# Attention and a low-rank mixer MLP: from two phases in turn to one woven pass

## The chip, the cores and the metric

The kernel runs on one core of a Trainium2 chip. The metric is the device time of one execution in microseconds (us), as the median over several executions. TensorE does the matmuls, VectorE and ScalarE read their results, GpSimd and SyncE here mostly start transfers. In the profile lines these are PE (matmuls), PEld (loads of a matmul's stationary operand, "weights"), DVE, ACT, POOL and SP. A line number such as L215 is that of the kernel that was profiled.

## The reference

The batch is 8; each has 12 heads of 448 rows and 64 columns. The head outputs, side by side, are the 448 x 768 input of a mixer.

```python
def rmsnorm(x, g):
    return x / np.sqrt(np.mean(x * x, axis=-1, keepdims=True) + 1e-06) * g
q_n, k_n = rmsnorm(q, g_q), rmsnorm(k, g_k)
attn = softmax(q_n @ k_n.T / 8)             # per batch and head, 448 x 448
x = concat_heads(attn @ v)                  # 448 x 768
u = x + ((x.T @ U) @ V).T                   # U 448 x 32, V 32 x 448: mixes rows
out = u + np.maximum(u @ w_ch1, 0) @ w_ch2  # 768 -> 3072 -> 768
```

Inputs and output are 32-bit floats; both kernels multiply in bf16 and accumulate in 32 bits.

## The kernel before

There are two phases. Attention of all 8 batches writes its result, transposed, to a scratch tensor in device memory. Then the weights are loaded and the MLP of all batches runs. A scheduler orders the instructions from their dependences and buffers.

```python
# phase 1, for each batch (rmsnorm: Square, sum, Copy, reciprocal, Sqrt, multiply)
for h in range(H):
    for (src, gs, tg) in [(qnb, g_qs, "qT"), (knb, g_ks, "kT")]:
        ... # 4 transposes of 112x64, then ScalarE copies with the gain
    avT = psum3.tile([D + 1, S], FP32, tag="avT")
    for ki in range(NSP):                                       # 4 key tiles of 112
        nc.tensor.matmul(sc, knT[:, ki*SP:(ki+1)*SP], qnT, start=True, stop=True)
        nc.scalar.activation(sce, sc, AF.Exp, scale=scal)       # 112 x 448
        nc.tensor.matmul(avT, va_all[:, ki, h, :], sce, ...)    # output transposed, 65 x 448
    nc.vector.reciprocal(den, avT[D:D + 1, :])                  # one row of 448
    nc.gpsimd.partition_broadcast(denb, den)
    nc.vector.tensor_mul(oT, avT[:D, :], denb)
    nc.sync.dma_start(x_scratch[b, h*D:(h+1)*D, :], oT)
# phase 2: load and cast the weights, then for each batch
#   read xT back, transpose it, mix, w1 and Relu, w2 and add, transpose, store
... # cut
```

The softmax here doesn't subtract the row's maximum and nothing guards it: scores larger than these inputs give would overflow.

## Time and profile before

| what | value |
|---|---|
| time, median of 4 | 1168.05 us |
| attention, from the slices | to about 590 us |
| weights arrive and TensorE has gaps | 590 to 730 us |
| one MLP batch, period in the timeline | 63 us |
| busy share of TensorE, VectorE, ScalarE | 86%, 52%, 43% |

First, the slices on the page of the kernel before. Each digit is the busy share of one fortieth of the span, in tenths. PEclk is the clock that the throttle's records grant.

```profile
PE   0888788788988899999744996999999999999997
DVE  3688989998788769667754121330212212130302
ACT  3677877777676665666400421004040312112130
PEclk9999999999999999999996898899999999999998
```

Attention is the first half: all three engines are busy together. The MLP is the second, and TensorE is alone. The chain of work that ended last, followed back over the whole span, on the same page:

```profile
PE 69%; ACT 9%; DMA 8%; issue 7%; DVE 5%; POOL 1%; SPq 0%; POOLq 0%; ACTq 0%; DVEq 0%
```

The timeline of TensorE gives its real speed. The columns are start, length, engine, line, operation, output and inputs, shapes, and how many were merged. The first line is from attention, the others from the MLP.

```profile
407.10 1.81 PE L109 MATMUL avT<-sce,va_all 112*65 112x448 bf16 x4
...
858.56 1.30 PE L184 MATMUL ph_6153<-uTb,w1b 128*128 128x448 bf16 x6
859.70 1.30 PE L184 MATMUL ph_6161<-uTb,w1b 128*128 128x448 bf16 x6
```

In the MLP six matmuls of 448 columns start every 1.14 us, 189 ns each. In attention the first three of the four shown start 380 and 373 ns apart, about 375 ns each (the fourth came later). So attention runs at half speed. The PEclk row prints 9s there because the trace holds no clock record before 617 us; the spacing of back-to-back matmuls is the safer reading. The Trainium skill, "TensorE: Matmul & The Clock Gate", Part 1, describes the two speeds, 1.2 and 2.4 GHz, and says that sustained activity lifts the clock. By these rates I estimate 373 and 187 ns for 448 columns, which agrees with the spacings.

One group of VectorE is large (columns: line, engine, operation, tiles, shapes, count; busy us and mean ns; idle time before and who ended it):

```profile
L111 DVE RECIPROCAL den<-avT 1x448 f32<-1x448 f32 x96 | 281.9, 2944 | 80.3 <-PE avT L109 79.1
```

### The profile page before, as it was taken

How to read it: one execution, taken by the hardware profiler on the slowest of the kernel's cores; microseconds unless marked ns; L12 is line 12 of the kernel's file. 1: busy time of each engine (PE TensorE's matmuls, PEld its weight loads, DVE VectorE, ACT ScalarE, POOL GpSimd, SP SyncE). 2: the span in 40 equal slices, each digit the busy share in tenths (PEclk: the TensorE clock that was granted, in tenths of full speed). 3: DMA queues.
4: the chain of work that ended last, by engine and by line, in shares of the span. 5: the costliest groups of instructions: out<-in, count | busy, mean ns of one | idle time of the engine just before them, and what ended most of it. 6: DMA issues, size and time to landing. Idle time of an engine off the chain costs nothing.

```text
span 1165.7 us, 11492 instructions
## 1 busy us (share of the span) xinstructions
PE 1004.5 (86%) x4424; PEld 457.6 (39%) x4424; DVE 601.6 (52%) x483; ACT 495.7 (43%) x847; POOL 94.3 (8%) x122
## 2 busy tenths in 40 slices
PE   0888788788988899999744996999999999999997
PEld 0333233333333333333221443455555555555553
DVE  3688989998788769667754121330212212130302
ACT  3677877777676665666400421004040312112130
POOL 0012312211111111111110000000000000000000
PEclk9999999999999999999996898899999999999998
DMA  9567766243260000000075334011010202010101
GB/s 179 96 105 129 127 117 117 53 96 58 45 120 8 13 10 12 13 12 8 12 260 191 109 109 127 18 42 41 1 48 1 71 1 71 1 48 1 48 1 48
DMA packets 153703, 74.79 MB, mean 64 GB/s; under 512 B 133904, under 2 KB 146224, under 8 KB 152880
## 3 DMA queue, kind: packets, MB, share of 16 engines
q1 hardware_dynamic: 153648, 74.06, 27.7%
q8 instruction: 34, 0.56, 0.2%
q14 instruction: 21, 0.17, 0.0%
HBM read 57.52 MB, written 16.52 MB: 64 GB/s over the span
## 4 chain that ended last, share of the span: by engine, by line
PE 69%; ACT 9%; DMA 8%; issue 7%; DVE 5%; POOL 1%; SPq 0%; POOLq 0%; ACTq 0%; DVEq 0%
PE po L192 18%; PE sc L106 13%; PE avT L109 13%; DMA wf<-in_moe_w_ch_dram 7%; PE pt L97 6%; ACT sce L108 4%; PE ph L176 3%; ACT tT L99 2%; PE ot L198 2%; DVE w2b L136 1%; ACT L77 1%; ACT L108 1%; DVE ob L79 1%; DVE den L111 1%; DVE w1b L132 1%
## 5 line engine op out<-in xcount | busy, mean ns | idle before, releaser
L111 DVE RECIPROCAL den<-avT 1x448 f32<-1x448 f32 x96 | 281.9, 2944 | 80.3 <-PE avT L109 79.1
L108 ACT ACTIVATE sce<-sc 112x448 bf16<-112x448 f32 x384 | 200.0, 542 | 158.3 <-PE sc L106 115.3
L192 PE MATMUL po<-hT,w2b 128*128 128x448 bf16 x1152 | 231.5, 356 | 13.1 <-DVE w2b L136 12.9
L109 PE MATMUL avT<-sce,va_all 112*65 112x448 bf16 x384 | 196.1, 571 | 46.4 <-ACT sce L108 43.8
L106 PE MATMUL sc<-tT 64*112 64x448 bf16 x384 | 217.1, 599 | 14.2 <-ACT sce L108 13.1
L195 DVE TENSOR_TENSOR ofin<-po,uTb 128x448 bf16<-128x448 f32 x48 | 29.9, 625 | 312.2 <-PE po L192 312.2
L184 PEld LDWEIGHTS <-w1b 128*128 128x128 bf16 x1152 | 113.3, 99 | 125.6 <-DVE w1b L132 17.5
L192 PEld LDWEIGHTS <-w2b 128*128 128x128 bf16 x1152 | 110.3, 98 | 115.7 <-DVE w2b L136 19.9
L97 PE MATMUL pt<-ident,ob 112*64 112x112 bf16 x768 | 103.4, 292 | 40.1 <-DVE ob L79 31.4
L106 PEld LDWEIGHTS <-tT 64*112 64x112 bf16 x384 | 61.2, 178 | 168.1 <-issue 160.0
L113 POOL PARTITION_BROADCAST denb<-den x96 | 86.4, 900 | 461.6 <-DVE den L111 461.5
L97 PEld LDWEIGHTS <-ob 112*64 112x64 bf16 x768 | 74.3, 159 | 121.2 <-PE sc L106 42.5
L109 PEld LDWEIGHTS <-va_all 112*65 112x65 bf16 x384 | 51.3, 146 | 102.4 <-issue 85.1
L115 DVE TENSOR_TENSOR oT<-avT,denb 64x448 bf16<-64x448 f32 x96 | 59.2, 617 | 18.2 <-POOL denb L113 16.8
L99 ACT ACTIVATE tT<-pt,g_ks 64x448 bf16<-64x448 bf16 x96 | 59.7, 622 | 8.0 <-PE pt L97 4.3
L74 DVE TENSOR_REDUCE ssq<-sq 112x48 f32<-112x3072 f32 x16 | 53.0, 3311 | 19.1 <-ACT sq L72 19.1
L99 ACT ACTIVATE tT<-pt,g_qs 64x448 bf16<-64x448 bf16 x96 | 59.5, 620 | 3.0 <-PE pt L97 1.9
L79 DVE TENSOR_TENSOR ob<-t,ssq 112x3072 bf16<-112x3072 f32 x16 | 53.2, 3325 | 1.4 <-ACT ssq L77 1.4
L136 DVE CAST w2b<-wf 128x768 bf16<-128x768 f32 x24 | 13.4, 560 | 65.6 <-DMA wf<-in_moe_w_ch_dram 65.6
L176 PE MATMUL ph<-Wb,xb 112*128 112x448 bf16 x192 | 44.2, 368 | 1.2 <-DVE uTb L178 0.6
L72 ACT ACTIVATE sq<-t 112x3072 f32<-112x3072 f32 x16 | 44.1, 2754 | 0.0
L199 DVE CAST osb<-ot 112x512 f32<-112x512 bf16 x48 | 33.1, 690 | 21.1 <-PE ot L198 21.1
(420 smaller groups left out, 599.4 us busy)
## 6 DMA issues: line engine op xcount, KB each, us to landing
t<-in_q_dram SPq DMA_DIRECT2D x32, 336.0 KB, 5.1
t<-in_k_dram SPq DMA_DIRECT2D x32, 336.0 KB, 5.3
vt<-in_v_dram SPq DMA_DIRECT2D x32, 336.0 KB, 5.8
out_dram<-osb SPq DMA_DIRECT2D x32, 336.0 KB, 4.2
wf<-in_moe_w_ch_dram SPq DMA_DIRECT2D x6, 1536.0 KB, 6.7
wf<-in_moe_w_ch_dram SPq DMA_DIRECT2D x24, 384.0 KB, 3.0
x_scratch<-oT SPq DMA_DIRECT2D x96, 56.0 KB, 1.9
xT<-x_scratch SPq DMA_DIRECT2D x8, 672.0 KB, 4.8
```

Of the source, the lines that this page charges most:

```text
L79: nc.vector.tensor_tensor(ob, t, ssq.rearrange("p a h -> p a h ()").to_broadcast([SP, NSP, H, D]), AluOpType.mult)
L97: nc.tensor.transpose(pt[:, si * SP:(si + 1) * SP], src[:, si, h, :], ident[:SP, :SP])
L99: nc.scalar.activation(tT, pt, AF.Copy, scale=gs)
L106: nc.tensor.matmul(sc, knT[:, ki * SP:(ki + 1) * SP], qnT, start=True, stop=True)
L108: nc.scalar.activation(sce, sc, AF.Exp, scale=scal)
L109: nc.tensor.matmul(avT, va_all[:, ki, h, :], sce, start=(ki == 0), stop=(ki == NSP - 1))
L111: nc.vector.reciprocal(den, avT[D:D + 1, :])
L113: nc.gpsimd.partition_broadcast(denb, den)
L115: nc.vector.tensor_mul(oT, avT[:D, :], denb)
L176: nc.tensor.matmul(ph, xb[:, si, dti * P:(dti + 1) * P], Wb[:, si, :], start=(si == 0), stop=(si == KS - 1))
L184: nc.tensor.matmul(ph1, w1b[:, dti, hti * P:(hti + 1) * P], uTb[:, dti, :], start=(dti == 0), stop=(dti == KD - 1))
L192: nc.tensor.matmul(po, w2b[:, hti, dti * P:(dti + 1) * P], hT[:, hti, :], start=(hti == 0), stop=(hti == KH - 1))
```

## The change

The intent is to keep TensorE working on the MLP while the other engines serve attention. Attention of batch b+2 is cut into pieces, and these are placed by hand between chunks of six MLP matmuls of batch b. To fit, most pieces were rewritten: two heads at once in scores and transposes; the value product turned round, so that its output needs no scratch tensor (the mixing transposes it by matmuls against the identity); the mixing done in its low-rank form and the second MLP product turned round too, so that the output needs no transposes; 1/rms as exp(-0.5 ln(.)), from the one table that also serves the softmax; weights cast by the transfers. Two batches share the row tiles, so an even batch's MLP works on 384 rows and the next on 512. The diff, cut to its core:

```diff
-    # two phases, ordered by the scheduler
+    nc.scalar.preload_act_table_set("natural_log_exp_and_others")
+    def stats(t):                       # one tile t: four heads of q and k
+        ...  # Square on ScalarE, sums on VectorE
+        nc.scalar.activation(rs, rs, AF.Ln, bias=eps)
+        nc.scalar.activation(rs, rs, AF.Exp, scale=-0.5)
+    def scores(p, kcs):                 # p: a pair of heads
+        for kc in kcs:
+            for hh in range(2):
+                pp = slice(hh * D, (hh + 1) * D)       # rows 0-63 or 64-127
+                nc.tensor.matmul(sc[:, hh, 0:S], kT[pp, kc*SP:(kc+1)*SP], qT[pp, :], ...)
+    def values(p, hh):
+        for i, off in enumerate(OFFS[par]):            # 4 tiles of 128 query rows
+            for kc in range(NJ):
+                nc.tensor.matmul(o[:, i, :], E[:, hh, c:c + P], va[:, hl, kc, :], ...)
+        nc.vector.reciprocal(rec, o[:, :, D])          # 128 x 4
+        ...                                            # scale into x3 and xs
+    def mlp(b):                         # yields after each chunk of six matmuls
+        ...
+    def attention(b):                   # pieces, in this order, for each pair p
+        # start(p): scores 0, 1, exp 0 | values(p-1, 0) | exp 1 | [even p: stats(t+1)]
+        # scores 2, 3, exp 2 | values(p-1, 1) | exp 3 | [odd p: scale(t+1)] | transposes(p+1)
+    def weave(fill, total, items):      # spreads the items evenly over MLP columns
+        ...
+    with tc.manual_schedule():
+        ...                             # batch 0's attention alone
+        for b in range(B):
+            fill, total = mlp(b), volume(b % 2)
+            if b == 0:
+                first = attention(1)
+                for _, piece in first[:6] + mixing(0):
+                    piece()
+                weave(fill, 24 * 384, first[6:])
+                weave(fill, total - 24 * 384 - 3000, attention(2))
+            else:
+                weave(fill, total * 0.84, attention(b + 2) ...)
+            weave(fill, total * 0.13, mixing(b + 1))
```

## The prediction

> **What bounds the kernel now.** Two phases run in turn. In the 40 slices, attention fills the first half (to about 590 us), then weights load and the MLP runs to the end. The chain of waits is 69% TensorE. The timeline shows two TensorE speeds. In the MLP a 448-column matmul follows the last after 189 ns, a 128-column transpose after 56 ns. In attention three back-to-back avT matmuls are 375 ns apart: half speed for 560 us, although the page's clock row prints 9s there. The Trainium skill, "TensorE: Matmul & The Clock Gate", Part 1, says the array runs at 1.2 GHz until sustained activity lifts it to 2.4; these spacings agree. So attention costs twice what its columns need, and every change between a score (K=64) and another matmul adds about 0.18 us (spacing 0.55 instead of 0.375). One MLP batch takes 63 us, so 8 take about 505 us.
>
> **What the change does to TensorE**, at the fast clock (columns/2.4 GHz + 2.5 ns, which gives the measured 189 and 56):
> - MLP: the same 1.03 M columns in 2496 matmuls: 436 us.
> - Low-rank mixing (mix_t, mix_u, V4 terms): 35 us; output and x transposes go.
> - Values turned round: 1536 matmuls of 65 columns, bound by their 128-column weight loads; I take 65 ns (the 56 ns transposes have such loads): 100 us.
> - Transposes, two heads at once: 384 x 56 ns = 21 us.
> - Scores: 384 x 448 columns in two row halves. The skill's "TensorEngine Tiling (Array Packing)", Key Properties, says tiles run in parallel and a change of tiling mode drains the array; no run here shows the parallelism. 36 us, plus four changes per pair of 0.17 us: 33 us.
>
> Sum about 660 us, all critical. The rest hides if the weave works: ScalarE about 290 us (a 448-column exp is 542 ns, so 896 columns about 0.92 us, x192, plus squares and half the relus), VectorE about 350 us. The 2.94 us one-row reciprocals (282 us of VectorE), broadcasts, scratch round trip, weight-cast copies and repeated table loads go; most was not on the chain.
>
> **On top.** First TensorE work at about 15 us (24.3 now). Batch 0's attention runs alone, at half speed and latency-bound: about 9 us a pair instead of 5, +24 us. Stalls in the weave (transposes directly followed by the scores that need them, the 2.6 us scale before its transposes, the single bank shared by values and transposes, batch 0's MLP carrying two attentions, the weights' arrival): about 55 us. Tail 4 us. Total about **755 us**, range 700 to 840. Chances: faster 0.97, within 2% 0.02, slower 0.01.
>
> **What would show the steps right.** 384-column matmuls near 162 ns apart from about 80 us on (fast clock throughout the weave); values 56 to 80 ns apart; four scores in about 0.4 us; TensorE above 75% of the chain; batches 6 and 7 (no attention) about 55 and 64 us, woven ones 85 to 105; ScalarE and VectorE each below 60% busy; one table load.
>
> **What would make it wrong.** If the weave's short matmuls let the clock fall to half, the time goes above 1000. If score pairs do not overlap, +36 us. If a weight load does not hide under 65 columns, values cost 100 ns each, +55 us. If the casting loads of the weights come late, +10 to 30 us. If stalls are nearly nil, about 700.

## The result, and the profile after

The changed kernel takes 720.83 us (median of 4, 720.27 to 721.71). The kernel before took 1168.05 us. The ratio is 0.6173, with a 95% interval from 0.6164 to 0.6182. The time is inside the predicted range, 34 us below its centre.

The slices after, with the same meaning:

```profile
PE   1606787878899999989999999989999999999997
DVE  3425655656555545645556544654555333233211
ACT  2615455555354530664165322554255211101200
PEclk9999799989999999999999999999999999999999
```

From the twelfth slice on TensorE is busy nearly all the time, while VectorE and ScalarE do attention beside it. The losses are in the first quarter. The chain after:

```profile
PE 71%; DVE 17%; ACT 5%; DMA 4%; issue 2%; ACTq 0%; SPq 0%; DVEq 0%
```

A piece of the weave in the timeline of TensorE:

```profile
299.79 1.15 PE L276 MATMUL ph<-uA,w1b 128*128 128x384 bf16 x6
300.78 0.67 PE L215 MATMUL o<-va_97,E_95 112*128 112x65 bf16 x16
301.29 3.09 PE L276 MATMUL ph<-uA,w1b 128*128 128x384 bf16 x18
304.21 0.56 PE L180 MATMUL pt<-ident,qkn 112*128 112x112 bf16 x8
304.61 1.14 PE L276 MATMUL ph<-uA,w1b 128*128 128x384 bf16 x6
306.61 0.59 PE L194 MATMUL sc<-qT,kT 64*112 64x448 bf16 x4 [0.86 <-DVE kT L185]
307.12 1.15 PE L276 MATMUL ph<-uA,w1b 128*128 128x384 bf16 x6
```

Read the starts. Six MLP matmuls of 384 columns take 0.99 us, about 163 ns each, which is full speed. Sixteen value matmuls take 0.51 us (32 ns each), eight transposes 0.40 us, four scores 0.51 us. A pair of heads needs two score calls, two value calls and one set of transposes: 2.46 us of TensorE. There is a wait of 0.86 us where scores follow their transposes with too little between.

The costliest single wait is early:

```profile
39.09 9.06 ACTq L112 DMA_DIRECT2D Uf<-in_moe_U_dram  x13
48.19 3.24 ACTq L115 DMA_DIRECT2D Vf<-in_moe_V_dram  x4
51.37 0.29 DVE L113 CAST Ub<-Uf 128x256 bf16<-128x256 f32 x1 [12.53 <-DMA Vf<-in_moe_V_dram]
...
54.19 0.38 DVE L185 COPY kT<-pt 128x448 bf16<-128x448 bf16 x1
54.62 0.99 PE L194 MATMUL sc<-qT,kT 64*112 64x448 bf16 x4 [14.79 <-DVE kT L185]
```

ScalarE spends 12 us starting small transfers of U and V, and VectorE waits in order for them. The copies of q and k for the next pair (L185 is that of k) come after that cast in the program and ran only after it, at 54 us, so TensorE is idle for 14.8 us.

TensorE's time can now be booked:

| stretch | time |
|---|---|
| first TensorE work | at 14.7 us |
| batch 0's attention alone and its mixing, at half speed | 14.7 to 89 us, 14.8 of it the gap above |
| batch 0's MLP, with two attentions | 89 to 200 us |
| batches 2 and 4, woven | 72 us each |
| batches 1, 3 and 5, woven | 85 us each |
| batch 6, no attention pieces but the last two | 52 us |
| batch 7, alone, and the end | 650 to 719 us |

Batch 7's matmuls take about 64 us and it has no mixing to carry (2.8 us). So six pairs add 85 - 64 - 2.8, about 18 us, to an odd batch: 3 us a pair. Batch 6, with its mixing but without the last two pieces (1 us), takes 50.7 us, so six pairs add 21 us to batches 2 and 4: 3.5 us a pair. A pair alone takes about 8 us in batch 0.

### The profile page after: what moved, and what is told of

The parts are those of the page before. It is cut to its first block, busy times and chain, and to the rows that moved or that the text cites. A ratio compares the mean times of both kernels' runs of the same rounds, so it can differ in the third digit from the quotient of the medians.

```text
span 719.2 us, 12074 instructions
## 1 busy us (share of the span) xinstructions
PE 629.4 (88%) x5168; PEld 357.1 (50%) x5168; DVE 342.7 (48%) x773; ACT 272.0 (38%) x385; POOL 80.4 (11%) x126
## 4 chain that ended last, share of the span: by engine, by line
PE 71%; DVE 17%; ACT 5%; DMA 4%; issue 2%; ACTq 0%; SPq 0%; DVEq 0%
PE po L296 28%; PE ph L276 24%; DVE qkn L168 7%; PE sc L194 6%; PE o L215 6%; DVE rstd L155 5%; ACT E_95 L199 2%; PE pt L180 2%; DMA qk<-in_k_dram 2%; ACT sq L154 2%; DVE qT L184 1%; PE pu L256 1%; PE pu L253 1%; PE po L294 1%; DMA gk_93<-in_g_k_dram 1%
## 5 line engine op out<-in xcount | busy, mean ns | idle before, releaser
L296 PE MATMUL po<-w2b,hT 128*128 128x384 bf16 x1344 | 246.1, 328 | 0.0
L296 PEld LDWEIGHTS <-hT 128*128 128x128 bf16 x1344 | 125.8, 98 | 81.9 <-issue 9.5
L276 PE MATMUL ph<-uB,w1b 128*128 128x512 bf16 x576 | 133.4, 379 | 0.0
L199 ACT ACTIVATE E_95<-sc 112x896 bf16<-112x896 f32 x96 | 84.8, 911 | 78.2 <-PE sc L194 66.2
L281 DVE TENSOR_SCALAR hT<-ph 128x384 bf16<-128x384 f32 (+1 forms) x96 | 59.8, 623 | 101.1 <-PE ph L276 100.7
L199 ACT ACTIVATE E_96<-sc 112x896 bf16<-112x896 f32 x96 | 84.8, 914 | 51.8 <-PE sc L194 51.8
L276 PE MATMUL ph<-uA,w1b 128*128 128x384 bf16 x576 | 104.0, 326 | 0.1
L194 PE MATMUL sc<-qT,kT 64*112 64x448 bf16 x384 | 66.0, 410 | 40.3 <-DVE kT L185 34.3
L168 DVE TENSOR_TENSOR qkn<-qk,rstd 112x512 bf16<-112x512 f32 x96 | 59.7, 682 | 1.0 <-ACT rstd L159 0.7
L147 POOL DMA_DIRECT2D va_99<-in_v_dram x32 | 22.5, 704 | 177.2 <-PE o L215 170.8
L215 PEld LDWEIGHTS <-E_95 112*128 112x128 bf16 x768 | 33.1, 103 | 10.4 <-issue 3.2
L215 PEld LDWEIGHTS <-E_96 112*128 112x128 bf16 x768 | 32.7, 103 | 10.8 <-issue 3.6
L147 POOL DMA_DIRECT2D va_98<-in_v_dram x32 | 22.5, 704 | 134.4 <-PE o L215 134.4
L147 POOL DMA_DIRECT2D va_97<-in_v_dram x32 | 22.6, 708 | 132.4 <-PE o L215 128.6
```

The source lines that it names most:

```text
L147: nc.gpsimd.dma_start(va[:, h, :, 0:D], v[b, h0 + h].rearrange("(p j) d -> p j d", j=NJ))
L168: nc.vector.tensor_tensor(qkn[:, pr, s].rearrange("p j h d -> p h j d"), qk[:, s, hp].rearrange("p h (j d) -> p h j d", d=D), rstd[:, s, h ...
L194: nc.tensor.matmul(sc[:, hh, 0:S], kT[pp, kc * SP:(kc + 1) * SP], qT[pp, :], start=True, stop=True)
L199: nc.scalar.activation(Es[p % NE][:, :, PAD + kc * S:PAD + (kc + 1) * S], scs.pop((p, kc))[:, :, 0:S], AF.Exp, scale=float(D) ** 0.5)
L215: nc.tensor.matmul(o[:, i, :], E[:, hh, c:c + P], va[:, hl, kc, :], start=(kc == 0), stop=(kc == NJ - 1))
L276: nc.tensor.matmul(ph, w1b[:, dc, hc * P:(hc + 1) * P], u[:, dc, :], start=(dc == 0), stop=(dc == KD - 1))
```

## The experiments

Three theories are possible for the 447 us. A: the weave hides attention's waits behind the MLP. A1: within that, it is the clock that matters, because the MLP's matmuls keep TensorE at full speed. B: the pieces themselves are cheaper, and the order adds little.

### 1. All pieces, no weave (e1_no_weave)

```diff
-                weave(fill, total * 0.84, att)
-            weave(fill, total * 0.13, mixing(b + 1))
-            for _ in fill: pass
+            for _, piece in att: piece()
+            for _ in fill: pass
+            for _, piece in mixing(b + 1): piece()
```

> The changed kernel with every piece kept, but not woven: the attention of batch b+2 runs as one block, then the MLP of batch b, then the mixing. Theory A (the weave is the largest part: it hides attention's waits and keeps TensorE fast): each head pair takes the 8 us it takes in batch 0 of the changed kernel, 48 x 8 = 384 us, plus MLP and mixing 470 us, plus 30 us of start: 870 to 900 us, with scores and values at half speed in most blocks. Rival B (the cheaper attention pieces are the gain, the weave adds little): under 780 us.

It took 905.44 us, ratio 0.7763, just above A's 870 to 900 us and far from B's 780. So the new pieces give 262 of the 447 us, and the weave the other 184: neither theory alone accounts for the whole gain. By stages of the two profiled runs, attention falls from 590 us to 401 us (the sum of its blocks), and the rest from 576 to 497 us, where the weights come early and x and the output need fewer transposes. The timeline of an attention block in this run:

```profile
256.17 0.99 PE L194 MATMUL sc<-qT,kT 64*112 64x448 bf16 x4 [0.84 <-DVE kT L185]
257.10 1.06 PE L215 MATMUL o<-va,E 112*128 112x65 bf16 x16
258.09 1.14 PE L194 MATMUL sc<-qT,kT 64*112 64x448 bf16 x4
259.16 1.06 PE L215 MATMUL o<-va,E 112*128 112x65 bf16 x16
261.86 1.16 PE L180 MATMUL pt<-ident,qkn 112*128 112x112 bf16 x8 [1.64 <-DVE qkn L168]
264.44 0.99 PE L194 MATMUL sc<-qT,kT 64*112 64x448 bf16 x4 [1.43 <-DVE kT L185]
```

From one first score call to the next is 8.3 us, at half speed, with over 3 us of waits for VectorE. Before, a pair took 11.7 us (the one-row reciprocals, one for each head, start 5.83 us apart from 200 to 400 us).

### 2. No weave, but the clock held up (e2_no_weave_spin)

```diff
+    def spin(n):                                   # ones: 128 x 384, no one reads pd
+        for _ in range(n):
+            nc.tensor.matmul(pd, ones[:, 0:P], ones, start=True, stop=True)
             for _, piece in att:
                 piece()
+                spin(2)
```

> As the run without the weave, plus two useless 128x384 matmuls after each attention piece, which use only idle TensorE time and a free bank. Theory A1 (half of the loss without the weave is the slow clock): the added matmuls hold the clock at full speed, a pair falls from 8 to about 6 us, and the total is 60 to 100 us below the run without the weave although TensorE has more to do. Rival (the loss is the chain of waits between engines, the clock only follows): within 25 us of it, or slower by the added 2.5 to 5 us per pair.

It took 890.37 us, 15 us less than without, although TensorE had more to do. The clock in the profiled run rose from 0.848 to 0.959. But the first score calls of neighbouring pairs still lie 7.8 us apart in the median, where they were 8.1 (36 spacings in each run from about 80 us on, without those across an MLP). So A1's size falls, and the rival's forecast (within 25 us) holds: what the weave hides is mostly the chain of waits between engines, and the clock's net part in it is small. The added work may hide some of the clock's worth; the 15 us are a net figure.

### 3. The clock in the kernel before (e3_before_spin, e5_before_spin_tied)

```diff
 # e3, after each value matmul
+                    nc.tensor.matmul(pd, ones[:, 0:P], ones, start=True, stop=True)
 # e5, instead, so that it can't run before the exp
+                    for _ in range(2):
+                        nc.tensor.matmul(pd, ones[:SP, :], sce, start=True, stop=True)
```

> The kernel before, with one useless 128x448 matmul of 128 rows after each value matmul in attention. If these raise the clock to full speed and TensorE was what bound attention, the 560 us fall to 350 or less. If they raise the clock but VectorE binds next (480 of its 560 us are busy there), only to about 500 us: total 1090 to 1120. If the clock stays at half speed, 384 x 0.375 us are added: total 1240 to 1310.

It took 1172.55 us, 0.6% more, and is inconclusive as it was meant: the added matmuls depend on nothing, and the scheduler put all 384 of them before 130 us. It still shows one thing. While they ran, the clock was full, and when they ended it was at half for 488 us. Attention alone, with TensorE 80 to 95% busy in stretches of 100 us, never lifted it. (VectorE's busy time, 464 us of the first 590 before, is a little less than this forecast and the next say.)

> The kernel before with two useless matmuls (128 columns of weights, 448 moving) on each exp tile in attention, so that the scheduler cannot move them to the start as it did in the first try. Theory (the slow clock is a symptom in attention: VectorE, 85% busy with its 2.94 us reciprocals, and the exp chain set the pace): the clock turns full, and attention keeps about 5.8 us a head, so the total stays within 1130 to 1190 us. Rival (the half clock set the pace): attention falls below 4.5 us a head and the total below 1050 us. If the clock stays at half speed: above 1300 us.

It took 1236.00 us, which is none of the three forecasts. The clock went up and down. Three stretches of this run, with the number of one-row reciprocals (one for each head) in the brackets after DVE busy; the columns are the stretch and its length, DVE and POOL busy, granted clock, DMA share, GB/s:

```profile
384.00:428.00 44.00, 23.18 (x8) 5.15 (x7) 1.00 0.55 105
428.00:472.00 44.00, 16.18 (x7) 4.42 (x6) 0.50 0.03 7
473.00:620.00 147.00, 88.93 (x31) 25.01 (x30) 1.00 0.05 13
```

The counts take in heads that lie only partly in a stretch. By the starts of the reciprocals a head takes 5.8, 8.3 and 4.8 us in the three stretches. Each has eight useless matmuls in it, 1.5 us at full clock and 3.0 us at half. It has to be compared with the same heads of the kernel before, because these too get faster later on, when fewer transfers run. There they take 5.8, 6.1 and 5.3 us, at half clock and without the useless matmuls. Two views with the same 30 heads (60 to 90; the count of POOL), first of this run:

```profile
488.00:631.30 143.30, 88.42 (x31) 25.00 (x30) 1.00 0.05 13
```

Then of the kernel before, where the 1.00 only means that no clock record was kept:

```profile
397.00:556.50 159.50, 88.60 (x31) 22.03 (x30) 1.00 0.05 12
```

So my statement for this run, that the clock is only a symptom before, falls for these heads: full clock is worth 0.5 us a head, net of the useless matmuls. For the eight heads of the first stretch it is worth nothing, net. If all 96 heads gained as the last ones did, it would be some 50 us of attention's 560; that was not shown, and what the clock is worth without added work stays open. Most of attention's time stays at full clock too. The rival, below 4.5 us, is not reached either.

### 4. The table (e4_sqrt_table)

```diff
-        nc.scalar.activation(rs, rs, AF.Ln, bias=eps)
-        nc.scalar.activation(rs, rs, AF.Exp, scale=-0.5)
+        nc.scalar.activation(rs, rs, AF.Sqrt, bias=eps)
+        nc.vector.reciprocal(rs, rs)
```

> The changed kernel with 1/rms by Sqrt on ScalarE and a VectorE reciprocal instead of Ln and Exp: two table loads of 1.28 us per tile of four heads come back, 24 x 2.6 = 62 us of ScalarE, which is 38% busy. Theory A: each delays an exp and through it a score, so part of it shows: +10 to +30 us. Rival: ScalarE has slack enough, less than +5 us.

It took 742.56 us, 22 us more, ratio 0.6375. ScalarE became 57 us busier (from 272.0 to 329.5), and over a third of that reached the total. The Trainium skill, "ScalarE: Activation LUTs", section "What ACT_TABLE_LOAD costs", gives 1283 ns for a load; the 49 loads in the trace of this run took 1.28 us each, as those of the kernel before did. Who waited is not ScalarE's reader but the transposes. The waits of TensorE from 110 to 600 us, in us in total, times, longest; first the changed kernel:

```profile
PE pt L180 <- DVE xs_100 L222: 6.1, 4, 2.1
PE pt L180 <- DVE xs_101 L222: 4.5, 3, 1.9
```

Then the one with Sqrt:

```profile
PE pt L180 <- DVE xs L222: 19.8, 12, 2.9
```

A likely account is that VectorE, which ran its work in the program's order in the gap above, stands at a reciprocal or a sum that ScalarE delays, and meanwhile doesn't empty the bank that values and transposes share. That account fits these waits, which grow by 9 us, but it was not tested. By batches, 3 us of the loss lie before batch 0's MLP, 10 in it, where the clock fell more often in this run, and 7 in batches 1 to 5.

### 5. Weight loads of 127 columns (e6_weights_127)

```diff
-                nc.tensor.matmul(o[:, i, :], E[:, hh, c:c + P], va[:, hl, kc, :], ...)
+                m = P if kc == 0 else P - 1
+                nc.tensor.matmul(o[0:m, i, :], E[:, hh, c:c + m], va[:, hl, kc, :], ...)
```

> The changed kernel with 127 instead of 128 weight columns in three of four value matmuls; on purpose wrong in one row of 128. Theory (the fast weight load, which the Trainium skill's TensorE page gives to exactly 128 columns, is why a value matmul took 32 ns and not the 65 that were predicted): these 1152 matmuls go to 60 to 110 ns, total +30 to +85 us. Rival (the load simply takes 32 ns for so many columns): less than +5 us.

It took 742.71 us, 22 us more, and is wrong in one row of 128 on purpose. The theory holds, with a size below its forecast: a value matmul with 127 columns of weights starts 59 ns after the one before, one with 128 columns 32 ns after. 1152 x 27 ns are 31 us, and 22 of them show: in each of the batches 1 to 5, where 144 such matmuls cost 3.9 us, the batch takes 3.2 to 3.8 us longer. The groups of weight loads, first in this run (busy us, mean ns):

```profile
L216 PEld LDWEIGHTS <-E 112*127 112x127 bf16 x1152 | 93.6, 151 | 6.2 <-issue 0.2
```

Then one of the two E buffers of the changed kernel:

```profile
L215 PEld LDWEIGHTS <-E_95 112*128 112x128 bf16 x768 | 33.1, 103 | 10.4 <-issue 3.2 <-DVE xs_100 L222 1.4
```

The Trainium skill, "TensorE: Matmul & The Clock Gate", section "Weight-path perf modes", says that a fast weight load is used when the number of weights is 128 and the type is not 32-bit float. This run agrees, for 128 against 127 columns of bf16; no other width was tried. One column less costs nearly a factor of two.

### 6. Scores ordered by row half (e7_scores_by_half)

```diff
-        for kc in kcs:
-            for hh in range(2):  ...matmul(head hh, key tile kc)
+        for hh in range(2):
+            for kc in kcs:       ...matmul(head hh, key tile kc)
```

> The changed kernel with the four score matmuls of a call in the order head 0, head 0, head 1, head 1, so that neighbours share the row half twice and differ once. Theory (two row halves run at once): a call of four goes from 0.51 to about 0.70 us, 96 calls, +10 to +18 us. Rival (halves do not overlap, the 0.51 us comes otherwise): within 3 us.

It took 727.37 us, +6.5 us: between the two forecasts. The starts of the four matmuls of one call in the trace, in ns from the first, explain why:

```
changed kernel, usual call:       0    3   233   237
heads in order, most calls:       0    7   233   240
heads in order, one of the 17:    0  268   271   504
```

In the changed kernel the two heads start 3 ns apart, so the row halves do run at once, as the Trainium skill's "TensorEngine Tiling (Array Packing)", Key Properties, says. In the reordered kernel the same picture appears in 58 of the 82 calls after 90 us: the third matmul of the program starts 7 ns after the first, and the second only at 233 ns. The records tell them apart, because the second carries a wait and the third a signal. So TensorE let the other half's matmul pass the one whose half was still busy; that this is the reason is inferred. In 17 of the 82 calls the four start in the program's order, and the fourth comes alone, about 0.23 us after the third; in most of these the second started late. The other seven lie in between. The experiment could not switch the overlap off; that it exists is shown by the starts. By batches, 2.7 of the profiled run's 7.6 us are lost before batch 0's MLP, at half speed, 3.0 in it, and only 1.8 after it.

### 7. Three defects of the order (e8, e9, e10, e11)

The first edit takes the constants of the mixing off the two engines that attention needs:

```diff
-                    nc.scalar.dma_start(Uf[...], Ur[...])      # and Vf; then the casts
+                    nc.sync.dma_start(Uf[...], Ur[...])        # casts after batch 0's attention
```

> The changed kernel with the 18 small loads of the mixing constants issued by SyncE instead of ScalarE, and the VectorE casts that wait for them placed after batch 0's attention. Theory (the 14.8 us TensorE gap at 40 to 55 us is ScalarE issuing and VectorE waiting in order behind them): the gap goes, -11 to -15 us. Rival (the gap is the DMA engines full with weights at that time, and the next loads of q and k are late as well): less than -5 us.

It took 706.23 us, -14.6 us. The gap is gone: transposes at 38.57 us are followed by scores at 39.98. The rival, late loads of q and k, falls.

The second weaves one batch ahead instead of two:

```diff
-                weave(fill, 24 * 384, first[6:])
-                weave(fill, total - 24 * 384 - 3000, attention(2))
-            else: weave(fill, total * 0.84, attention(b + 2))
+            ahead = attention(b + 2)[:6]               # they hold the last values of b+1
+            weave(fill, total * 0.84, attention(b + 1)[6:] + ahead)
```

> The changed kernel with the attention of batch b+1, not b+2, woven into the MLP of batch b, so that batch 0's MLP carries one attention instead of two. Theory (of the 112 us from 88 to 200, only 81 are TensorE work, because 48 chunks cannot cover two attentions and the clock falls there three times): most of the 31 us come back, -15 to -25 us. Rival (these waits are the 2.5 us VectorE blocks and would appear anywhere in the weave): within 5 us.

It took 707.16 us, -13.7 us, just short of the forecast. The 31 us of idle time in batch 0 came back only in part, because the waits for VectorE moved into the other batches: batch 0's MLP became 38.7 us shorter, batch 6, which now carries an attention (14.8 us of TensorE work), 15.8 us longer, and batches 1 to 5 together 9 us longer (the clock fell once in each of four of them). The rival is not right, but it has a share.

> One batch ahead, the mixing constants loaded by SyncE, and the product of the two gains placed after the first scaling. If the two gains are independent: 720.8 less 14.6 less what one-ahead gives alone, so 680 to 692 us.

It took 690.49 us, -30 us, so the two gains add up. The placement of the two gains' product, which let the sums start at 5.6 us instead of 10.9, is in this number: batch 0's MLP starts 3.0 us earlier than in the run with the first edit alone.

```diff
 # even pair: squares and sums where they were; Ln and Exp after exp 3
-        stats: Square, sum, Ln, Exp in one piece
+        stats: Square, sum      ...      stats_exp: Ln, Exp
 # odd pair
-        ... exp 3 | scale(t+1) | transposes(p+1)
+        start(p) | scale(t+1) | values(p-1, 0) | ... | exp 3 | transposes(p+1)
```

> As the run with both fixes, plus the norm pieces moved: Ln and Exp half a pair after the squares and sums, so that ScalarE does not stand still for VectorE's 2.4 us of sums, and the 2.5 us scaling right after the odd pair's first scores, far from the transposes that need it. Theory (the waits of transposes for these VectorE blocks are most of what is left in batch 0's attention and the weave): a pair of batch 0 falls from 8 to 6.5 to 7 us, -6 to -15 us. Rival: the waits only move, within 3 us.

It took 659.19 us, ratio 0.5658 (0.5650 to 0.5667): 31 us less, twice the largest forecast. Its pairs in batch 0 fell only from 8 to 7.4 us, less than I thought. The rest of the gain is in the weave, 2 to 5 us in each of batches 0 to 6. The two moves of this run were not tried apart. Stretches of the run with both fixes (columns: stretch and length; busy us of PE, PEld, DVE, ACT, POOL, with counts; clock, DMA share, GB/s):

```profile
90.00:200.00 110.00, 104.97 (x870) 57.26 (x875) 60.18 (x130) 50.66 (x73) 11.95 (x17) 0.98 0.33 56
200.00:600.00 400.00, 385.15 (x3257) 220.22 (x3268) 211.19 (x482) 166.16 (x237) 36.58 (x52) 0.99 0.30 57
```

The same stretches of the run with the norm moved:

```profile
90.00:200.00 110.00, 108.80 (x929) 60.82 (x934) 61.84 (x137) 50.05 (x72) 12.65 (x18) 1.00 0.38 68
200.00:600.00 400.00, 395.10 (x3395) 227.89 (x3407) 218.48 (x496) 168.37 (x240) 35.17 (x50) 1.00 0.29 55
```

TensorE's idle time from 90 to 600 us falls from 20 to 6 us, and the clock never falls after 67 us, where it fell four times for 3.4 us. Batch 0's MLP takes 68 us; it took 110 us in the changed kernel, and 72 us once it carried one attention instead of two, so most of that is the second edit's.

### 8. The clock at the start (e12_spin_at_start)

The edit is spin(2), as in experiment 2, after each piece of batch 0's attention.

> As the run with the norm pieces moved (ratio 0.5658 to the kernel before), plus two useless 128x384 matmuls after each piece of batch 0's attention, the only stretch that still runs at half speed. Theory (that stretch is bound by the chain between engines; the clock is worth about 0.5 us a pair and the 2 us of slow mixing after it): -3 to -8 us, ratio 0.559 to 0.563. Rival (the added matmuls delay the chain as much as the clock speeds it): within 2 us, or slower.

It took 657.04 us, ratio 0.5643 (0.5633 to 0.5653). The clock was full from the first pairs on and they took 7.0 us instead of 7.4, but the total moved by 1.7 us by the ratios (2.2 by the medians), and the intervals overlap. The rival holds: not worth keeping.

## Why the prediction was right

The prediction named the bound, the mechanism and the risks rightly, and the time fell inside its range. Its sum had terms that were off and cancelled in part, and that is luck: with the cheaper TensorE work alone put right it would have been 680 us, below its range.

- **TensorE as the bound: right.** 384-column matmuls are 163 ns apart (162 predicted) in the weave. The chain is 71% TensorE, below the 75% said, because 17% hangs on VectorE, about half of it before 200 us (batch 0). ScalarE is 38% busy and VectorE 48%; one table load remains.
- **The values term was mis-sized.** The step was "bound by their 128-column weight loads; I take 65 ns": 100 us. It measured 32 ns, 49 us. Experiment 5 shows the cause: weight loads of exactly 128 columns are fast. The 65 ns would have been near right for 127 columns (59 ns). I had taken the rate from transposes that move 128 columns, and the moving side set their time: in the changed kernel transposes with such loads that move 112 columns are 49 ns apart, and values that move 65 are 32.
- **The scores term was mis-sized.** Parallel halves were right. Four mode changes of 0.17 us a pair were not: a call of four takes 0.51 us where its columns need 0.38, so the extra is 0.13 us for a call and about 0.26 us for a pair, not 0.68. 69 us became 49 us.
- **Batch 0's attention was mis-sized the other way.** Half speed and about 9 us a pair were right (53 us in six pairs, without the gap). But the 9 us were compared with 5 us at full clock, where a pair needs 2.46, and the 14.8 us gap was not seen. With slow mixing, "+24 us" is about 57 us.
- **Stalls and tail: right in size.** Predicted 59 us. From 89 us to the end are 630 us, of which TensorE's work at full speed is 568 (MLP 436, values, scores and transposes of 42 pairs 103, mixing 29): 62 us. About 31 of them are in batch 0's MLP, so most of the rest of the weave ran nearly without waits.
- The account: 755 predicted (its terms add to 758), -75 for cheaper TensorE work, +33 in batch 0's attention, +3 stalls, gives 716, and 719 were measured in the profiled run.
- **"Attention costs twice what its columns need"** is true before, but it suggested that the clock was the prize. Experiments 2 and 3 put the clock's worth, net of the matmuls that they add, at 15 us for the new pieces in blocks, and before at between nothing and 0.5 us a head, some 50 us in all at the most. The larger part of attention's time was waits between engines, and the weave hides those.
- **Woven batches were predicted at 85 to 105 us**, and took 72 and 85, for the reasons above.

What stays open is how the 262 us of experiment 1 split among the single rewrites (reciprocals, paired heads, no scratch tensor, early weights, mixing and output without their transposes). They were not undone one by one.

## What to carry to other kernels

A phase that waits on several engines and a phase that is bound by TensorE can be woven: a pair of heads that took 8 us alone added 3 to 3.5 us to the MLP, where its own TensorE work is 2.5 us. What a hand-made order then loses is mostly in-order engines standing at one wait while later work for others queues behind it; weaving one batch ahead, and moving a few VectorE and ScalarE pieces and small transfers away from their readers, took another 62 us (720.83 to 659.19). Read the speed of TensorE from the spacing of back-to-back matmuls, and cost each small matmul from an example with the same weight width.

## What the Trainium skill lacked or had wrong

- "TensorE: Matmul & The Clock Gate", Part 3, says that matmuls start and end in program order without reordering. In experiment 6 the third score matmul of a call, in the other row half, started 7 ns after the first and the second at 233 ns, in 58 of 82 calls.
- The same page, section "LDWEIGHTS (loading the stationary operand)", gives columns/1.2 ns, which is 106 ns for 127 columns. That fits at half speed (107 ns between value matmuls that each have such a load), but at full speed they are 59 ns apart. With 128 columns, the case that the page calls fast, they are 54 and 32 ns apart, near what their 65 moving columns take at the measured rates (375 and 189 ns for 448 columns: 54 and 27 ns).
- The same page, section "Back-to-back issue gap", gives about 131 ns for 512-column matmuls in a stream with weight loads. Here 472 of the 576 first-layer matmuls of 512 columns, each with its own load, start 215 or 216 ns after the one before.
- The same page, Part 1, doesn't say how busy counts as busy (Part 4 only that transposes count differently). The attention before kept TensorE about 80 to 95% busy with 64-row scores, 65-column values and transposes and stayed at half speed for 560 us; two matmuls of 112 x 128 weights on each exp tile lifted it only part of the time.
- "TensorEngine Tiling (Array Packing)", Key Properties, names the drain on a change of tiling mode, but gives no time. Here a call of four scores takes 0.13 us more than its columns, with both changes and the weight loads in it.
